# Moving the first layernorm's normalisation from GpSimd to VectorE and ScalarE in a linear-attention block with a gated MLP

## The chip, the cores and the metric

The kernel runs on one core of a Trainium2 chip. The metric is the device time of one execution in microseconds; the median of several runs is compared. The core has TensorE (PE, matrix products), VectorE (DVE), ScalarE (ACT), GpSimd (POOL) and SyncE (SP, which only issues DMAs here). TensorE writes its products to eight PSUM banks; the others bring them from there to on-chip memory (SBUF).

## What is computed

```python
def _layernorm(x, axis=-1, eps=1e-5):
    m = jnp.mean(x, axis=axis, keepdims=True)
    v = jnp.var(x, axis=axis, keepdims=True)
    return (x - m) / jnp.sqrt(v + eps)

def _A_ref(x, wqkv, wo):                      # H = 32 heads of 32
    q, k, v = ...                             # x @ wqkv, split
    phi = lambda t: jnp.where(t > 0, t + 1, jnp.exp(t)) + 1e-6
    pq, pk = phi(q), phi(k)
    kv = jnp.einsum("bhsd,bhse->bhde", pk, v)
    z = jnp.einsum("bhsd->bhd", pk)
    num = jnp.einsum("bhqd,bhde->bhqe", pq, kv)
    den = jnp.einsum("bhqd,bhd->bhq", pq, z)[..., None] + 1e-6
    return merge_heads(num / den) @ wo

def _B_ref(x, W_gate, W_up, W_down):
    gate = jnp.einsum("bsd,df->bsf", x, W_gate)
    up = jnp.einsum("bsd,df->bsf", x, W_up)
    gate = gate * (gate > 0)
    return jnp.einsum("bsf,fd->bsd", gate * up, W_down)

h  = x + _A_ref(_layernorm(x), wqkv, wo)
h2 = h + _B_ref(_layernorm(h), W_gate, W_up, W_down)
```

There are 2048 tokens of width 1024, and the hidden width of the MLP is 3584. All inputs and the output are bf16.

## The kernel before

**Stages.** The tokens are cut into tiles of 128 rows, 16 in all. The first layernorm (class `Norm`, L644) takes them in pairs: tile t of the first half of the tokens and tile t + 8 of the second. K and V are computed pair by pair, and K^T V is accumulated in PSUM (the K/V stage). The Q stage follows, together with the attention tiles (class `Tile_`, L1004): each divides by the denominators, multiplies by wo, adds x, and applies the second layernorm. Then come gate and up, then down.

**Products.** Most products use a fast scheme with seven products in place of eight on 2x2 blocks (class `Quad`, L326). It needs sums and differences of blocks of the left operand (`left_sums`, L621) and of the weights (`WForms.sums`, L596, and others), all made by VectorE. A quad takes three PSUM banks A, D and E. p1 writes A, and ScalarE copies it to D (`fork`). p6 adds to A, and ScalarE copies the result out (`snap`, u2). p5 writes E; p7 adds to A, and that is copied out too (u3). p2 adds to D. Then an output is made from E and u3 (c22), and only when E has been read may p3 add to it. p4 adds to A. p4 and p3 of a quad are issued after p1 of the next.

**The first layernorm.** Its statistics are computed in two ways. Most tiles of the first half use VectorE (`bn_stats`, `bn_aggr`). Tiles with `on_act` use ScalarE: a Copy pass whose accumulator gives the sum, then, once the negated mean is known, a Square pass with that as its bias, whose accumulator gives the variance. `neg` (L656) computes the negated mean on GpSimd, for both kinds. `rstd_` (L678) does Ln and Exp on ScalarE. `finish` (L696) applies the two: GpSimd does (x + (-mean)) * rstd for twelve tiles, VectorE for tiles 1 and 9. Tiles 0 and 8 have their own path (`apply_first`, L685), with the mean itself, on VectorE. A DMA transpose then puts the tile into XI, from where TensorE reads it. The second layernorm (`Tile_.norm`, L1074) has its own code and applies on GpSimd.

**The order of the work.** The program is not issued as it is written. Class `Plan` (L33) records every instruction as a node with its predecessors, an estimated duration (`hold`) and a due time (`late`, from TensorE's order and the successors). `schedule` (L202) then runs a list schedule on a clock of its own, in nanoseconds, and the instructions are issued in that order; on the chip each engine takes its own in order. On an engine other than TensorE the ready node with the earliest due time is taken; but the engine may be held idle for a node that is not yet ready, if that becomes ready within a part of the candidate's duration and is due more than 1500 ns earlier. That part is `(1.2 if s < self.SHORT else 0.5) * v.hold` (L246), with `SHORT = 215000.0` on the planner's clock.

**The attention tiles.** `tiles` (L1089) lists 16 of them; `steps` (L1094) makes the program's order from the list, one tile behind another. Index `i` is the half of the tokens, `s` the half within that, `tt` the tile within 512 columns. The first eight (s = 0) run during the Q stage, and their second layernorm must be in XI before the first gate products. In `norm` a tile with i = 1 also asks for left sums: with tt = 1 for columns 0 and 1 together (four sums of 128x1024), with tt = 2 and 3 for one each (four of 128x512).

Of the kernel before, what the change touches and what calls it, by code (L numbers as in the profile page):

```python
# [8 lines left out]
ACT = mybir.ActivationFunctionType  # L9
ALU = mybir.AluOpType  # L10
# [22 lines left out]
class Plan:  # L33
# [6 lines left out]
    WINDOW = 6000.0  # L40
    AHEAD = 120000.0
    OPENING = 45000.0
    SHORT = 215000.0

    class Node:
        __slots__ = ("eng", "calls", "preds", "hold", "lat", "open", "dma", "late", "ready", "left", "start", "nom")
# [155 lines left out]
    def schedule(self):  # L202
        nodes = self.nodes
        succs = self.order()
        engines = ("tensor", "vector", "scalar", "gpsimd", "sync")
        avail = {e: [] for e in engines}
        clock = {e: 0.0 for e in engines}
        for i, v in enumerate(nodes):
            v.left, v.ready = len(v.preds), max(0.0, v.late - self.AHEAD) if v.dma else 0.0
            if v.eng != "tensor" and v.late > 2.0 * self.OPENING:  # L210

                v.ready = max(v.ready, self.OPENING)
            if not v.left:
                avail[v.eng].append(i)
        pe = [i for i, v in enumerate(nodes) if v.eng == "tensor"]
        done, first, wire, out = set(), 0, 0.0, []
        while True:
            best = None
            for e in engines:
                a = avail[e]  # L220
                if not a:
                    continue
                if e == "sync":
                    for i in a:
                        v = nodes[i]
                        if v.late - max(clock[e], v.ready) > 6000.0:
                            v.ready = max(v.ready, wire - 2000.0)
                if e == "tensor":
                    while first < len(pe) and pe[first] in done:
                        first += 1  # L230
                    limit = nodes[pe[first]].nom + self.WINDOW
                    a = [i for i in a if nodes[i].nom <= limit]
                    if not a:
                        continue
                s = max(clock[e], min(nodes[i].ready for i in a))
                if best is None or s < best[0]:
                    best = (s, e, a)
            if best is None:
                break
            s, e, a = best  # L240
            now = [i for i in a if nodes[i].ready <= s]
            i = min(now, key=lambda i: (nodes[i].nom if e == "tensor" else nodes[i].late, i))
            v = nodes[i]
            if e != "tensor":

                wait = (1.2 if s < self.SHORT else 0.5) * v.hold  # L246
                soon = [j for j in a if s < nodes[j].ready < s + wait and nodes[j].late < v.late - 1500.0]
                if soon:
                    i = min(soon, key=lambda j: (nodes[j].late, j))
                    v = nodes[i]  # L250
                    s = v.ready
            v.start = s
            clock[e] = s + v.hold
            end = s + v.hold + v.lat
            if v.dma:
                wire = max(wire, s + v.hold) + v.dma
                end = wire + v.lat - v.dma + min(4000.0, max(0.0, 0.25 * (v.late - s)))
            elif e == "sync":

                end = max(end, min(wire + 800.0, end + 2500.0))  # L260
            avail[e].remove(i)
            done.add(i)
            out.append(i)
            for j in succs[i]:
                w = nodes[j]
                r = clock[e] if w.eng == e else end
                w.ready = max(w.ready, r)
                w.left -= 1
                if not w.left:
                    avail[w.eng].append(j)  # L270
        assert len(out) == len(nodes)
        self.span = max(clock.values())
        return out
# [205 lines left out]
def block_kernel(ctx: ExitStack, tc: tile.TileContext, x, wqkv, wo, wg, wu, wd, out, H: int):  # L479
    nc = tc.nc  # L480
    P = 128
    xf = x.flatten_outer_dims()
    of = out.flatten_outer_dims()
    S, D = xf.shape
# [9 lines left out]
    SW = 512  # L494
    NS = 2
# [45 lines left out]
    def scratch(tag, n):  # L541

        if tag not in tiny_rings:
            tiny_rings[tag] = [0, tiny_at[0]]
            tiny_at[0] += 4 * n
            assert tiny_at[0] <= 208
        r = tiny_rings[tag]
        r[0] += 1
        lo = r[1] + (r[0] % 4) * n
        return tiny[:, lo:lo + n]  # L550
# [16 lines left out]
    hw, nc = nc, Plan(nc)  # L567
# [69 lines left out]
    def load_x(t):  # L637
        p, i = t % NP, t // NP
        x_tiles[t] = at(190 + 4 * (p % 2) + 2 * i, [D])
        nc.sync.dma_start(out=x_tiles[t], in_=xf[t * P:(t + 1) * P, :])  # L640
# [3 lines left out]
    class Norm:  # L644
# [8 lines left out]
            else:  # L653
                self.stats = scratch("stats", 2 * 6).rearrange("p (a b) -> p a b", b=6)

        def neg(self, src, by):  # L656
            self.negm = scratch("negm", 1)
            nc.gpsimd.tensor_scalar(out=self.negm[:], in0=src, scalar1=by, scalar2=None, op0=ALU.mult)

        def stat(self, j):  # L660
            if not self.on_act:
                nc.vector.bn_stats(out=self.stats[:, j, :], in_=self.x[:, j * 512:(j + 1) * 512])
            elif j == 0:
                nc.scalar.activation(out=self.xn, in_=self.x, func=ACT.Copy, accum_out=self.sm[:, 0:1])
                self.neg(self.sm[:, 0:1], -1.0 / D)
            else:
                nc.scalar.activation(out=self.xn, in_=self.x, func=ACT.Square, bias=self.negm[:], scale=1.0,
                                     accum_out=self.sm[:, 1:2])

        def aggr(self, first=False):  # L670
            if self.on_act:
                return
            self.mv = mv = scratch("mv", 2)
            nc.vector.bn_aggr(out=mv[:], in_=self.stats[:])
            if not first:
                self.neg(mv[:, 0:1], -1.0)

        def rstd_(self):  # L678
            lnv = scratch("lnv", 1)
# [13 lines left out]
            for k in range(2):  # L693
                nc.scalar.copy(out=XH[self.i][k][:, :, self.r:self.r + P], in_=pt[:, k * KH:(k + 1) * KH, :])

        def finish(self, on_dve=False):  # L696
            self.rstd_()
            xn = self.xn
            (nc.vector if on_dve else nc.gpsimd).tensor_scalar(out=xn, in0=self.x, scalar1=self.negm[:], scalar2=self.rstd[:],
                                    op0=ALU.add, op1=ALU.mult)  # L700
            nc.sync.dma_start_transpose(out=XI[self.i][:, :, self.r:self.r + P], in_=xn)
            if self.t == ST - 1:
                nc.follow(nc.last())
                for k, h in W_ORDER:
                    WQ.load(k, h)
                nc.follow(None)
            if self.t % NP + 2 < NP:
                load_x(self.t + 2)
# [83 lines left out]
    def v_quad(p):  # L792
        v = v_ring()

        def blk(i, j):
            return v[:, i, j * KH:(j + 1) * KH, 0:P]

        def copy(i, j):
            return lambda ps: nc.scalar.copy(out=blk(i, j), in_=split(ps))

        def add(i, j):
            return lambda ps, u: nc.vector.tensor_tensor(out=blk(i, j), in0=split(ps), in1=split(u), op=ALU.add)

        return v, Quad(tok_prod(p, WV), fork, snap,
                       {"c11": copy(0, 0), "c12": add(0, 1), "c21": copy(1, 0), "c22": add(1, 1)}, five_banks)
# [31 lines left out]
    def plain_k(i, j):  # L837
        k_phi(i, j, plain(WK, i, j))
# [38 lines left out]
    n0, n8, n1, n9 = Norm(0), Norm(8), Norm(1), Norm(9, True)  # L877
    for n in (n0, n8):
        n.stat(0)
        n.stat(1)  # L880
        n.aggr(first=True)
        n.rstd_()
        n.apply_first()
    n0.transpose_first()
# [4 lines left out]
        n.stat(1)  # L889
        n.aggr()  # L890
    plain_k(0, 0)
    n1.finish(True)
    n9.finish(True)
    tick.bg.extend(ks)
    tick()
    plain_k(1, 0)
# [15 lines left out]
    for p in range(1, NP):  # L912
# [6 lines left out]
        v, vq = v_quad(p)  # L919
# [166 lines left out]
                return (lag_s[0], chain_of(*left_sums(self.s * SW + (self.tt + 1 - n) * P, n * P)))  # L1086

    lag_s, turned = [3], []
    tiles = [Tile_(s, i, tt) for s in range(NS) for tt in range(SW // P) for i in range(2)]  # L1089

    def w(m, j):
        return lambda: tiles[m].wo(j)
# [440 lines left out]
@with_exitstack  # L1533
def kernel(
    ctx: ExitStack,
    tc: tile.TileContext,
    A_x: bass.AP,
    A_wqkv: bass.AP,
    A_wo: bass.AP,
    B_x: bass.AP,  # L1540
    B_W_gate: bass.AP,
    B_W_up: bass.AP,
    B_W_down: bass.AP,
    out: bass.AP,
):
    block_kernel(tc, A_x, A_wqkv, A_wo, B_W_gate, B_W_up, B_W_down, out, H=32)
# [30 lines left out]
```

## Time and profile before

| What | us |
|---|---|
| median of 8 runs | 726.82 (726.63 to 726.96) |
| the profiled execution, device time | 726.68 |
| its span, first to last instruction | 724.9 |

Every group of instructions has the same line (L123, the helper that issues recorded calls), so groups are told apart by engine, operation and shape. Some groups around the layernorm, over the whole span: count, busy us, mean ns of one.

| Engine and operation | Count | Busy us | Mean ns |
|---|---|---|---|
| POOL TENSOR_SCALAR 128x1024 (both layernorms) | 28 | 40.9 | 1461 |
| POOL TENSOR_SCALAR 128x1 (negated means) | 14 | 5.1 | 364 |
| DVE TENSOR_SCALAR 128x1024 with tiny operands | 4 | 2.2 | 546 |
| ACT ACTIVATE 128x1, tiny from tiny | 64 | 12.7 | 202 |

Busy time in windows of the first part, us:

| Window | PE | DVE | ACT | POOL |
|---|---|---|---|---|
| 20 to 40 | 18.58 | 17.53 | 15.49 | 8.13 |
| 40 to 60 | 18.07 | 15.30 | 14.86 | 8.60 |
| 60 to 80 | 20.00 | 15.77 | 16.10 | 5.91 |
| 80 to 100 | 20.00 | 14.55 | 10.29 | 0.81 |

The first layernorm's GpSimd applications run from 25.6 to 80.8 us and those of the second from 159.2 us on.

### The profile page before, as it was taken

The page shows a single profiled execution, that of the slowest core. Times are in us where ns is not written, and L with a number is a line of the kernel's source. Part 1 is how long each engine was busy: PE and PEld are TensorE (multiplying, and loading weights), DVE is VectorE, ACT ScalarE, POOL GpSimd, SP SyncE. Part 2 cuts the span into 40 slices and gives each one's busy share as a digit, 9 for nine tenths or more (in the row PEclk, how much of TensorE's full clock was granted, in tenths as well). Part 3 has the DMA queues.
Part 4 walks back from the last instruction along what each step waited for, and adds up shares of the span by engine and source line. Part 5 has one row for each costly group of instructions (what it writes and reads, how often), then busy time and mean ns, then how long its engine had stood idle before and what let it go on. Part 6 is the DMA issues. An engine that isn't in the chain of part 4 may idle for free.

```text
span 724.9 us, 11231 instructions
## 1 busy us (share of the span) xinstructions
PE 714.0 (98%) x4163; PEld 396.9 (55%) x4163; DVE 566.3 (78%) x954; ACT 277.2 (38%) x540; POOL 81.6 (11%) x88
## 2 busy tenths in 40 slices
PE   8998999999999999999999999999999999999998
PEld 3444545444444444444444444444444688888887
DVE  6887765788897965566766968769858879899996
ACT  5777654665655343333333333333333220001100
POOL 1343100002201220000000000000000004001452
PEclk9999999999999999999999999999999999999999
DMA  9544805249955540446145584686681868777973
GB/s 290 145 91 101 199 2 185 50 93 211 203 119 146 131 102 1 128 141 182 59 144 180 171 257 139 205 254 185 200 262 51 276 263 207 218 265 237 245 78 59
DMA packets 156503, 117.40 MB, mean 162 GB/s; under 512 B 54944, under 2 KB 140192, under 8 KB 156320
## 3 DMA queue, kind: packets, MB, share of 16 engines
q1 hardware_dynamic: 148832, 113.01, 53.5%
q0 software_dynamic: 7616, 3.67, 4.8%
q8 instruction: 32, 0.52, 0.3%
q14 instruction: 23, 0.19, 0.1%
HBM read 70.52 MB, written 34.08 MB: 144 GB/s over the span
## 4 chain that ended last, share of the span: by engine, by line
PE 87%; DVE 2%; ACT 2%; issue 1%; DMA 0%; POOL 0%; ACTq 0%; DVEq 0%
PE psum L123 87%; DVE mem L123 2%; ACT mem L123 1%; DMA mem<-mem 0%; ACT tiny L123 0%; ACT psum L123 0%; DVE tiny L123 0%; POOL tiny L123 0%; ACTq L123 0%; DVEq L123 0%
## 5 line engine op out<-in xcount | busy, mean ns | idle before, releaser
L123 PE MATMUL psum<-mem 128*128 128x512 bf16 (+4 forms) x4147 | 713.1, 335 | 7.4 <-ACT mem L123 2.6
L123 PEld LDWEIGHTS <-mem 128*128 128x128 f16 (+1 forms) x4163 | 396.9, 98 | 324.1 <-issue 10.8
L123 DVE TENSOR_TENSOR mem<-psum,mem 128x512 f32<-128x512 f32 (+2 forms) x240 | 187.1, 793 | 102.2 <-ACT mem L123 71.0
L123 DVE TENSOR_TENSOR mem<-mem 128x512 f16<-128x512 bf16 (+8 forms) x400 | 244.0, 650 | 7.9 <-DMA mem<-mem 2.8
L123 ACT COPY mem<-psum 128x512 f32<-128x512 f32 (+2 forms) x124 | 92.8, 750 | 215.3 <-PE psum L123 211.1
L123 ACT COPY psum<-psum 128x512 f32<-128x512 f32 (+1 forms) x68 | 49.1, 722 | 158.3 <-PE psum L123 156.1
L123 POOL DMA_DIRECT2D out_dram<-mem x28 | 34.1, 1299 | 412.1 <-DVE mem L123 412.0
L123 POOL TENSOR_SCALAR mem<-mem,tiny 128x1024 bf16<-128x1024 bf16 x28 | 40.9, 1461 | 181.7 <-ACT tiny L123 168.8
L123 ACT ACTIVATE mem<-psum 128x512 bf16<-128x512 f32 x90 | 53.6, 597 | 18.8 <-PE psum L123 18.2
L123 DVE SCALAR_TENSOR_TENSOR mem<-mem 128x512 bf16<-128x512 bf16 (+1 forms) x71 | 57.3, 806 | 1.2
L123 DVE SCALAR_TENSOR_TENSOR mem<-psum,mem 128x512 bf16<-128x512 f32 x66 | 45.2, 687 | 12.5 <-PE psum L123 10.2
L123 DVE TENSOR_SCALAR mem<-mem 128x512 bf16<-128x512 bf16 (+1 forms) x49 | 17.2, 354 | 19.9 <-ACT mem L123 19.3
L123 ACT ACTIVATE mem<-mem,tiny 128x1024 bf16<-128x1024 bf16 x24 | 27.5, 1145 | 8.4 <-DVE tiny L123 5.9
L123 DVE TENSOR_TENSOR mem<-psum,tiny 128x384 bf16<-128x384 f32 (+1 forms) x48 | 22.8, 507 | 4.3 <-ACT tiny L123 3.9
L123 ACT ACTIVATE mem<-mem 128x1024 bf16<-128x1024 f32 (+1 forms) x23 | 24.3, 1056 | 2.9 <-DVE mem L123 2.7
L123 ACT ACTIVATE tiny<-tiny 128x1 f32<-128x1 f32 (+2 forms) x112 | 22.5, 206 | 6.6 <-DVE tiny L123 3.8
L123 ACT ACTIVATE tiny<-psum 128x12 f32<-128x12 f32 (+1 forms) x48 | 8.1, 170 | 17.5 <-PE psum L123 17.2
L123 DVE BATCH_NORM_STATS2 tiny<-mem 128x6 f32<-128x512 bf16 x16 | 10.3, 683 | 2.4 <-DMA mem<-in_A_x_dram 2.4
L123 ACT CAST mem<-psum 128x512 bf16<-128x512 f32 x18 | 10.6, 588 | 4.2 <-PE psum L123 3.7
L123 POOL TENSOR_SCALAR tiny<-tiny 128x1 f32<-128x1 f32 x14 | 5.1, 364 | 38.8 <-ACT mem L123 21.4
L123 ACT ACTIVATION_READ_ACCUMULATOR mem<-mem,tiny 128x1 f32 x24 | 4.5, 188 | 0.0
L123 DVE TENSOR_SCALAR mem<-mem,tiny 128x1024 bf16<-128x1024 bf16 x4 | 2.2, 546 | 2.1 <-ACT tiny L123 1.5
(18 smaller groups left out, 15.6 us busy)
## 6 DMA issues: line engine op xcount, KB each, us to landing
l_dram<-mem SPq DMA_DIRECT2D x98, 128.0 KB, 2.3
mem<-l_dram SPq DMA_DIRECT2D x12, 896.0 KB, 6.3
mem<-in_A_x_dram SPq DMA_DIRECT2D x32, 256.0 KB, 3.0
mem<-in_B_W_up_dram SPq DMA_DIRECT2D x14, 512.0 KB, 5.4
mem<-in_B_W_gate_dram SPq DMA_DIRECT2D x14, 512.0 KB, 4.3
mem<-in_B_W_down_dram SPq DMA_DIRECT2D x28, 256.0 KB, 3.7
r_dram<-mem SPq DMA_DIRECT2D x56, 128.0 KB, 2.0
mem<-r_dram SPq DMA_DIRECT2D x8, 896.0 KB, 5.3
```

The costliest lines, as they stand in the source:

```text
L123: call = lambda: getattr(getattr(self.nc, eng), op)(*args, **k)
```

## The change

Four things. The hold of 1.2 durations applies only between 120 and 215 us of the planner's clock; before 120 us it is 0.5, as it already was after 215. The negated mean of the `on_act` tiles is computed by ScalarE, as a Copy with a scale; the other tiles use the mean itself and subtract. VectorE applies all tiles of `finish`. And the first eight attention tiles run all of i = 0 first, then all of i = 1, in place of alternating.

```diff
-    SHORT = 215000.0
+    MIXED = (120000.0, 215000.0)
...
-                wait = (1.2 if s < self.SHORT else 0.5) * v.hold
+                wait = (1.2 if self.MIXED[0] < s < self.MIXED[1] else 0.5) * v.hold
...
-        def neg(self, src, by):
-            self.negm = scratch("negm", 1)
-            nc.gpsimd.tensor_scalar(out=self.negm[:], in0=src, scalar1=by, scalar2=None, op0=ALU.mult)
-
         def stat(self, j):
             if not self.on_act:
                 nc.vector.bn_stats(out=self.stats[:, j, :], in_=self.x[:, j * 512:(j + 1) * 512])
             elif j == 0:
                 nc.scalar.activation(out=self.xn, in_=self.x, func=ACT.Copy, accum_out=self.sm[:, 0:1])
-                self.neg(self.sm[:, 0:1], -1.0 / D)
+                self.negm = scratch("negm", 1)
+                nc.scalar.activation(out=self.negm[:], in_=self.sm[:, 0:1], func=ACT.Copy, scale=-1.0 / D)
...
-        def aggr(self, first=False):
+        def aggr(self):
             if self.on_act:
                 return
             self.mv = mv = scratch("mv", 2)
             nc.vector.bn_aggr(out=mv[:], in_=self.stats[:])
-            if not first:
-                self.neg(mv[:, 0:1], -1.0)
...
-        def finish(self, on_dve=False):
+        def finish(self):
             self.rstd_()
             xn = self.xn
-            (nc.vector if on_dve else nc.gpsimd).tensor_scalar(out=xn, in0=self.x, scalar1=self.negm[:], scalar2=self.rstd[:],
-                                    op0=ALU.add, op1=ALU.mult)
+            by, op = (self.negm[:], ALU.add) if self.on_act else (self.mv[:, 0:1], ALU.subtract)
+            nc.vector.tensor_scalar(out=xn, in0=self.x, scalar1=by, scalar2=self.rstd[:], op0=op, op1=ALU.mult)
             nc.sync.dma_start_transpose(out=XI[self.i][:, :, self.r:self.r + P], in_=xn)
...
-    tiles = [Tile_(s, i, tt) for s in range(NS) for tt in range(SW // P) for i in range(2)]
+    tiles = [Tile_(0, i, tt) for i in range(2) for tt in range(SW // P)]
+    tiles += [Tile_(1, i, tt) for tt in range(SW // P) for i in range(2)]
```

More of the change, by code (lines that the diff above doesn't have):

```diff
@@ L880, in block_kernel @@
         n.stat(1)
-        n.aggr(first=True)
+        n.aggr()
         n.rstd_()
@@ L891, in block_kernel @@
     plain_k(0, 0)
-    n1.finish(True)
-    n9.finish(True)
+    n1.finish()
+    n9.finish()
     tick.bg.extend(ks)
```

## The prediction

> **What bounds the kernel now.** I read the page's list of busy times first, then TensorE's waits, its timeline, and the other engines around the two long gaps.
>
> ```profile
> PE 714.0 (98%) x4163; PEld 396.9 (55%) x4163; DVE 566.3 (78%) x954; ACT 277.2 (38%) x540; POOL 81.6 (11%) x88
> ```
> ```profile
> PE psum L123 <- ACT mem L123: 2.6, 2, 1.9
> PE psum L123 <- DVE mem L123: 2.1, 3, 1.4
> PE psum L123 <- DVE mem L558: 1.2, 1, 1.2
> PE psum L123 <- DMA mem<-mem: 0.6, 1, 0.6
> ```
> TensorE is idle for 724.9 - 714.0 = 10.9 us, and no change of other engines can win more. 3.5 of these follow its last matmul (721.35 to 724.9), 1.2 precede the first. Its timeline (columns: start, duration, what, idle before) has the rest:
>
> ```profile
> 10.49 18.29 PE L123 MATMUL psum<-mem 128*128 128x512 bf16 x84 [0.42 <-DMA mem<-in_A_wqkv_dram]
> 30.20 25.34 PE L123 MATMUL psum<-mem 128*128 128x512 bf16 x140 [1.42 <-DVE mem L123]
> 57.47 4.69 PE L123 MATMUL psum<-mem 128*128 128x512 f16 x21 [1.93 <-ACT mem L123]
> ...
> 171.95 4.94 PE L123 MATMUL psum<-mem 128*128 128x512 bf16 x28 [0.35 <-DVE mem L123]
> 177.24 30.61 PE L123 MATMUL psum<-mem 128*128 128x512 bf16 x152 [0.35 <-DVE mem L123]
> ```
> So the first layernorm's stretch holds two gaps, 1.42 us before 30.20 and 1.93 us before 57.47; the Q stage holds small ones (0.58 before 152.08 and the two of 0.35). From 270 to 721 TensorE runs without one. The change is worth what it does to the first two, less what it opens elsewhere.
>
> The gap before 57.47, on ScalarE and then on GpSimd:
>
> ```profile
> 52.38 0.57 ACT L123 COPY mem<-psum 128x512 f32<-128x512 f32 x1
> 54.89 1.15 ACT L123 ACTIVATE mem<-mem,tiny 128x1024 bf16<-128x1024 bf16 x1 [1.94 <-POOL tiny L123]
> ...
> 57.31 0.60 ACT L123 COPY psum<-psum 128x512 f32<-128x512 f32 x1
> ```
> ```profile
> 50.30 4.38 POOL L123 TENSOR_SCALAR mem<-mem,tiny 128x1024 bf16<-128x1024 bf16 x2
> 54.65 0.20 POOL L123 TENSOR_SCALAR tiny<-tiny 128x1 f32<-128x1 f32 x1
> ```
> The Square pass waits for a negated mean of 0.20 us, which stands on GpSimd behind two applications of 4.38 us. Behind the Square stand the copies that release TensorE: the delay is passed on whole (1.94 against 1.93).
>
> The gap before 30.20, on VectorE:
>
> ```profile
> 27.28 2.06 DVE L123 TENSOR_TENSOR mem<-mem 128x2048 f16<-128x2048 bf16 x1
> 29.27 0.28 DVE L123 TENSOR_SCALAR mem<-mem 128x512 bf16<-128x512 bf16 x1
> 29.47 0.68 DVE L123 TENSOR_TENSOR mem<-psum,mem 128x512 f32<-128x512 f32 x1
> ```
> TensorE waits for the add at 29.47, which reads bank E before p3 may add to it. Its other input, the copy u3, ended on ScalarE at 27.68: the add is late because weight sums stand before it. The last took 2.06 us, where the others take 1.22, beside a GpSimd application (28.27 to 30.54).
>
> **What the Trainium skill says.** "SBUF — State Buffer", section "Who interferes with whom": a VectorE operation with two SBUF inputs and a GpSimd operation that reads SBUF exclude each other for a whole instruction. The trace agrees: 2.06 against 1.22, and GpSimd's applications take 1.20 to 2.68 us. "TensorE: Matmul & The Clock Gate", the table of specifications: ScalarE's and VectorE's queues are strict FIFO. The trace agrees (ScalarE's 1.94 us above). "ScalarE: Activation LUTs", "Rules for kernel authors": about 0.3 us for an ACTIVATE besides its elements; the trace has 0.20 for a 128x1 one, and I use that.
>
> **The change part by part.**
> 1. *Twelve applications go from GpSimd to VectorE.* GpSimd loses 19.9 us (twelve at 1.665 mean up to 130 us). On VectorE four such stand in the trace:
>
> ```profile
> L123 DVE TENSOR_SCALAR mem<-mem,tiny 128x1024 bf16<-128x1024 bf16 x4 | 2.2, 546 | 2.1 <-ACT tiny L123 1.5 <-issue 0.5
> ```
> From start to next start one takes 0.46 (11.93 to 12.39). 12 x 0.46 = 5.5 us more. Less contention gives back 2.06 - 1.22 = 0.84 at 27.28 and 0.93 - 0.29 = 0.64 at 41.49: 1.5. Net 4.0. From 20 to 80 us VectorE is busy 17.53 + 15.30 + 15.77 = 48.6 of 60 (windows of 20 us); 52.6 fits, but the first window goes to about 18 of 20. On the chain to the next tile's transpose, 0.55 replaces 1.2 to 2.7, so the transposes go out 1 to 2 us sooner; TensorE waits for none there.
> 2. *Seven negations move to ScalarE, seven vanish.* ScalarE gains 7 x 0.20 = 1.4 us on 46.5 of 60, but no longer waits for GpSimd. At 52.4: the Square can start about 53.1 (after the copy, which ends at 52.95, and a negation of 0.20), not 54.89: 1.8 us of the 1.93 go. What is late next is ScalarE's own chain (Square, Ln, Exp, fork). Bounds: 0, if another wait takes its place, to 1.93. I take 1.8.
> 3. *The shorter hold before 120 us of the planner's time.* It costs nothing on the chip: it changes the order in which instructions are issued. VectorE stands idle for 2.19 us before 20.34, waiting for a transpose, with weight sums still to do. A hold of 0.5 in place of 1.2 durations lets one in (1.14 from start to start, 26.15 to 27.28). The other way, a long sum may now start in front of an urgent add. The add at 29.47 then: -0.84 (contention) -1.14 (idle time filled) +0.92 (two applications, ready at 25.4 and 28.0, in front of it) = 28.4; that takes 1.1 us of the 1.42. Bounds: +0.9 (applications before it, idle not filled, contention elsewhere) to -1.42. I take -1.0.
> 4. *Order of the first eight attention tiles.* Same work, other order. Left sums of columns 0 and 1 wait for the sixth tile, not the fourth: four sums of 0.68 move from 180-186 to after 188, those of column 2 (four of 0.42) about 3 us later. First gate products use them from about 204. VectorE's idle time is 13.00 - 10.14 = 2.9 in 187-200 and 8.00 - 7.62 = 0.4 in 200-208. 2.7 us fit, barely. Bounds -0.7 (both gaps of 0.35 closed, as VectorE is freer before 187) to +1.5. I take +0.2.
> 5. *New small stalls* from a fuller VectorE with more waits in 20-80: VectorE now stops for each rstd, with bank releases queued behind it. I take +0.2; its bad end is the second rival. The SP queue has the same transposes and loads, earlier; nothing is added to it. GpSimd's accumulating stores come after 600 us.
>
> Sum: -1.8 - 1.0 + 0.2 + 0.2 = -2.4 us. The profiled execution took 726.68 (span 724.9 and 1.8 around it): 724.3, span 722.5. The median before, 726.82, lies 0.14 higher: 724.4.
>
> **Rivals.**
> *Only one gap closes.* The first stays at 1.4, because the applications take the place of the contention, or the second turns into a wait for VectorE; gain 1.8 less small stalls of 0.8: 725.8. For it: VectorE is at 88% in 20-40. Against: the second gap's cause is removed by name.
> *VectorE as the bound (slower).* An application at the head of its queue waits for Ln and Exp on ScalarE, with bank releases behind it. The row above prices it: 2.1 us idle before four, 0.53 each; 12 x 0.53 = 6.3. Idle time left is 7.4 of 60 us. If half of the stops fall before an add that TensorE needs (3.2) and both applications at 25-29 do (0.9), less the 1.8 won: +2.3, 729.1. It decides once TensorE loses more than 1.8 to such stops. For it: ScalarE is busy 9.27 of 10 us in 20-30. Against: before a free VectorE comes to them, most rstd are long done.
> *All closes.* Both gaps (3.35) and the two of 0.35: 726.82 - 4.05 = 722.8. For it: both causes named above lie in what is removed. Against: closing the first needs VectorE to be free in its tightest window.
>
> **How the numbers follow.** Forecast 0.50 (own range 723.3 to 725.4), one gap 0.18, VectorE as bound 0.22, all 0.10. A measurement of this kernel tells about 0.2% (1.45 us) from no change, so "same" is 725.4 to 728.3. Faster: 0.50 + 0.10 = 0.60; same: 0.18 and a little of the third, 0.19; slower 0.21. Range: the low end is below "all closes" by a little, 722.4; the high end takes in one gap and the mild part of the third case, 728.5.
>
> **What would show it.** In the profile after: GpSimd has 16 applications and no 128x1 ones; no weight sum of 2 us; no wait of ScalarE for GpSimd's tiny tiles; TensorE's gap near 57 gone, that near 30 at 0.4 or less; the Q stage's within 0.5 of now. A wait of VectorE for ScalarE's tiny tiles that grows by several us, with TensorE waiting for VectorE from 20 to 80 us, would make it wrong; so would a gap before the first gate products near 204.

## The result

The changed kernel takes 724.5 us (median of 11 runs, 724.24 to 725.51) against 726.77 for the kernel before (31 runs): a ratio of 0.997, with a 95% interval of 0.9963 to 0.9978. The prediction said 724.4. The profiled execution took 724.65 us, its span is 722.9.

The page of the kernel after, list of busy times:

```profile
PE 714.1 (99%) x4163; PEld 396.6 (55%) x4163; DVE 569.6 (79%) x966; ACT 277.8 (38%) x548; POOL 56.7 (8%) x62
```

TensorE has the same work in a span shorter by 2.0 us. VectorE gained only 3.3 us of busy time for twelve more applications; GpSimd lost 24.9 and has 16 applications left and no negations. TensorE's waits, in the kernel after (total us, times, longest):

```profile
PE psum L123 <- DVE mem L123: 1.2, 4, 0.4
PE psum L123 <- DVE mem L558: 1.2, 1, 1.2
PE psum L123 <- ACT mem L123: 0.9, 2, 0.7
PE psum L123 <- DMA mem<-mem: 0.8, 1, 0.8
```

And its timeline:

```profile
10.45 43.96 PE L123 MATMUL psum<-mem 128*128 128x512 bf16 x224 [0.71 <-DMA mem<-in_A_wqkv_dram]
54.60 14.16 PE L123 MATMUL psum<-mem 128*128 128x512 f16 x76 [0.20 <-ACT mem L123]
68.91 13.18 PE L123 MATMUL psum<-mem 128*128 128x512 bf16 x72 [0.15 <-DVE mem L123]
82.47 47.77 PE L123 MATMUL psum<-mem 128*128 128x512 bf16 x267 [0.38 <-DVE mem L123]
...
149.94 19.52 PE L123 MATMUL psum<-mem 128*128 128x512 bf16 x112 [0.77 <-DMA mem<-mem]
169.81 4.94 PE L123 MATMUL psum<-mem 128*128 128x512 bf16 x28 [0.35 <-DVE mem L123]
175.10 30.75 PE L123 MATMUL psum<-mem 128*128 128x512 bf16 x152 [0.34 <-DVE mem L123]
```

The gap of 1.42 us is no longer a row of its own: one run of products goes from 10.45 to 54.41. The one of 1.93 is now 0.20. Two small ones, 0.15 and 0.38, are new, and the two in the Q stage stand as before. Together these come to -1.42 - 1.73 + 0.15 + 0.38 = -2.6. The wait for the first attention tile's transpose grew from 0.58 to 0.77, which leaves -2.4. The product behind that wait was, in the kernel before:

```profile
152.08 19.52 PE L123 MATMUL psum<-mem 128*128 128x512 bf16 x112 [0.58 <-DMA mem<-mem]
```

From the first product of the long run (10.49 and 10.45) to this one (152.08 and 149.94), TensorE takes 141.59 us before and 139.49 after: -2.1. The missing 0.3 went into stalls too short to be listed: up to the second place the products count as 43.96 us busy, where before they counted 18.29 + 25.34 = 43.63. This distance, called the stretch below, leaves out the start of the execution, which differs from run to run.

ScalarE at the second place, in the kernel after:

```profile
51.14 0.19 ACT L123 ACTIVATION_READ_ACCUMULATOR mem<-mem 128x1 f32 x1
51.23 0.19 ACT L123 ACTIVATE tiny<-tiny 128x1 f32<-128x1 f32 x1
51.32 0.57 ACT L123 COPY mem<-psum 128x512 f32<-128x512 f32 x1
51.79 0.21 ACT L123 ACTIVATE tiny<-tiny 128x1 f32<-128x1 f32 x1
52.03 1.15 ACT L123 ACTIVATE mem<-mem,tiny 128x1024 bf16<-128x1024 bf16 x1
...
54.45 0.59 ACT L123 COPY psum<-psum 128x512 f32<-128x512 f32 x1
```

The accumulator is read at 51.14, and the Square pass starts 0.89 us later; before, it was 52.28 and 54.89, 2.6 us. A negation of about 0.2 us on ScalarE itself is all that lies between besides other ready work. VectorE at the first place, in the kernel after:

```profile
25.70 1.22 DVE L123 TENSOR_TENSOR mem<-mem 128x2048 f16<-128x2048 bf16 x1
26.83 0.54 DVE L123 TENSOR_SCALAR mem<-mem,tiny 128x1024 bf16<-128x1024 bf16 x1
27.29 0.69 DVE L123 BATCH_NORM_STATS2 tiny<-mem 128x6 f32<-128x512 bf16 x1
27.89 0.28 DVE L123 TENSOR_SCALAR mem<-mem 128x512 bf16<-128x512 bf16 x1
28.08 0.69 DVE L123 TENSOR_TENSOR mem<-psum,mem 128x512 f32<-128x512 f32 x1
```

The add on which p3 waits starts at 28.08, not 29.47; one application and a statistics pass stand before it, and the last weight sum takes its plain 1.22 and starts 1.58 sooner (25.70 for 27.28).

### The profile page after: what moved, and what is told of

The parts are those of the page before. It is cut to its first block, busy times and chain, and to the rows that moved or that the text cites. A ratio compares the mean times of both kernels' runs of the same rounds, so it can differ in the third digit from the quotient of the medians.

```text
span 722.9 us, 11207 instructions
## 1 busy us (share of the span) xinstructions
PE 714.1 (99%) x4163; PEld 396.6 (55%) x4163; DVE 569.6 (79%) x966; ACT 277.8 (38%) x548; POOL 56.7 (8%) x62
## 4 chain that ended last, share of the span: by engine, by line
PE 87%; DVE 6%; ACT 3%; DMA 2%; issue 1%; SPq 0%; ACTq 0%; DVEq 0%
PE psum L123 87%; DVE mem L123 6%; ACT mem L123 3%; DMA mem<-in_A_wqkv_dram 1%; DMA mem<-mem 1%; DVE tiny L123 1%; ACT tiny L123 1%; SPq L123 0%; ACT psum L123 0%; ACTq L123 0%; DVEq L123 0%
## 5 line engine op out<-in xcount | busy, mean ns | idle before, releaser
L123 POOL TENSOR_SCALAR mem<-mem,tiny 128x1024 bf16<-128x1024 bf16 x16 | 20.9, 1309 | 243.3 <-ACT tiny L123 243.3
L123 ACT ACTIVATE tiny<-tiny 128x1 f32<-128x1 f32 (+2 forms) x120 | 24.0, 205 | 8.3 <-DVE tiny L123 5.3
L123 DVE TENSOR_SCALAR mem<-mem,tiny 128x1024 bf16<-128x1024 bf16 x16 | 8.5, 542 | 3.1 <-ACT tiny L123 3.1
L123 DVE TENSOR_SCALAR tiny<-tiny 128x1 f32<-128x1 f32 x16 | 3.4, 210 | 0.4
```

The costliest lines, as they stand in the source:

```text
L123: call = lambda: getattr(getattr(self.nc, eng), op)(*args, **k)
```

## The experiments

The change mixes where an operation runs with the order in which everything is issued, since the planner reads the engine and the hold. To part the two, the first experiments keep a kernel's order of issue to the instruction and only exchange the engine at the moment of issue: a recorded call may carry a substitute.

```diff
+        instead = k.pop("instead", None)
-        call = lambda: getattr(getattr(self.nc, eng), op)(*args, **k)
+        call = lambda: instead(self.nc) if instead else getattr(getattr(self.nc, eng), op)(*args, **k)
```

All were timed beside the kernel before. The table has their median time and its ratio to the kernel before (95% interval), and the stretch in the one profiled execution of each. Kernels that differ from one another only in the attention tiles agree in the stretch within 0.05 us (before and tiles_only; changed, after_old_tiles and second_on_vector; hold_from_60 and hold_60_second_vector), so it resolves more than the medians do, but nothing outside 10 to 152 us.

| Kernel | us | Ratio to before | Stretch, us |
|---|---|---|---|
| before | 726.77 | 1 | 141.59 |
| changed | 724.50 | 0.9970 (0.9963 to 0.9978) | 139.49 |
| neg_same_order | 724.83 | 0.9971 (0.9959 to 0.9982) | 139.40 |
| apply_same_order | 724.83 | 0.9970 (0.9960 to 0.9980) | 139.59 |
| both_same_order | 724.81 | 0.9969 (0.9957 to 0.9981) | 139.55 |
| hold_only | 725.99 | 0.9986 (0.9980 to 0.9993) | 141.33 |
| tiles_only | 726.65 | 0.9999 (0.9991 to 1.0007) | 141.57 |
| after_old_hold | 724.59 | 0.9971 (0.9961 to 0.9981) | 139.72 |
| after_old_tiles | 724.70 | 0.9970 (0.9959 to 0.9982) | 139.46 |
| after_apply_gpsimd | 728.83 | 1.0028 (1.0018 to 1.0038) | 143.77 |
| after_neg_gpsimd | 724.62 | 0.9973 (0.9961 to 0.9984) | 139.61 |
| second_on_vector | 723.99 | 0.9959 (0.9947 to 0.9972) | 139.51 |
| hold_from_60 | 723.88 | 0.9960 (0.9948 to 0.9973) | 138.61 |
| hold_60_second_vector | 722.80 | 0.9947 (0.9934 to 0.9961) | 138.66 |

### The engines alone, in the old order

**neg_same_order**: only the negations of the tiles with statistics on ScalarE move to ScalarE.

```diff
-            nc.gpsimd.tensor_scalar(out=self.negm[:], in0=src, scalar1=by, scalar2=None, op0=ALU.mult)
+            nc.gpsimd.tensor_scalar(..., **(dict(instead=lambda e: e.scalar.activation(
+                out=out, in_=src, func=ACT.Copy, scale=by)) if self.on_act else {}))
```

> The order of issue is that of the kernel before, and only the seven negations of the tiles with statistics on ScalarE are issued on ScalarE in place of GpSimd. Theory A (each gap has its local cause: the negation behind two applications makes the gap before 57.47): that gap falls from 1.93 to under 0.3 us, the one of 1.42 before 30.20 stays within 0.3; the time falls by 1.5 to 1.9, to about 725.1. Rival B (the gain comes from the planner's new order, and a wait that is removed alone is replaced by the next): the gap is replaced by another of 1 us or more and the time falls by less than 0.5.

TensorE's timeline in neg_same_order (its lines bear L124, as the substitute added one):

```profile
13.66 15.92 PE L124 MATMUL psum<-mem 128*128 128x512 bf16 x72
30.91 99.40 PE L124 MATMUL psum<-mem 128*128 128x512 bf16 x541 [1.33 <-DVE mem L124]
```

The second gap is gone from the list and the first stands at 1.33. The time falls by 2.1, a little more than the 1.5 to 1.9 expected, and the stretch by 2.2: seven moved instructions of 0.2 us, in an unchanged order, bring about as much as the whole change. Rival B falls.

**apply_same_order**: the twelve applications move to VectorE, and all negations stay.

```diff
-            (nc.vector if on_dve else nc.gpsimd).tensor_scalar(out=xn, in0=self.x, ...)
+            (nc.vector if on_dve else nc.gpsimd).tensor_scalar(out=xn, in0=x, ...,
+                instead=lambda e: e.vector.tensor_scalar(out=xn, in0=x, ...))
```

> The order of issue is that of the kernel before; the twelve applications are issued on VectorE in place of GpSimd, all negations stay on GpSimd. Theory A: no weight sum of 2 us is left, the negation near 54 no longer stands behind applications, so the gap before 57.47 falls below 0.5; the gap before 30.20 changes by -0.8 (contention gone) to +0.9 (two applications in front of the add); the time falls by 1 to 2.5, to 724.3 to 725.8. Rival B: VectorE in the old order stops at applications whose rstd is late, TensorE waits for VectorE by 1 us or more in 20 to 80, and the time is 726.5 or more.

```profile
13.79 15.06 PE L124 MATMUL psum<-mem 128*128 128x512 bf16 x68
29.05 1.02 PE L124 MATMUL psum<-mem 128*128 128x512 f16 x4 [0.20 <-ACT mem L124]
30.75 99.49 PE L124 MATMUL psum<-mem 128*128 128x512 bf16 x540 [0.67 <-DVE mem L124]
```

This is the same timeline for apply_same_order. The second gap goes here too, though the negation is still on GpSimd: what held it there was the queue in front of it. Of the first gap 0.20 + 0.67 = 0.87 are left. Rival B, VectorE as the bound in the old order, falls.

**both_same_order** joins the two edits.

> The order of issue is that of the kernel before; the applications go to VectorE and the seven negations to ScalarE. Theory A: nearly all of the changed kernel's gain without any new order: 724.4 to 725.2, TensorE's idle time from 20 to 80 us at most 1.2 (3.35 before). Rival B (new order needed): 725.8 or more.

724.81, within 0.02 of each alone. The two edits do not add up, since either one removes the same cause of the second gap: a small instruction that others wait for, behind long ones on GpSimd. What the applications do to the first gap as well (a few tenths) is too small for the medians. The gap before 30 is 1.04 here. VectorE's part shows why it is 0.38 lower than before:

```profile
28.68 0.54 DVE L706 TENSOR_SCALAR mem<-mem,tiny 128x1024 bf16<-128x1024 bf16 x1
29.14 0.28 DVE L124 TENSOR_SCALAR mem<-mem 128x512 bf16<-128x512 bf16 x1
29.34 0.68 DVE L124 TENSOR_TENSOR mem<-psum,mem 128x512 f32<-128x512 f32 x1
29.94 0.54 DVE L706 TENSOR_SCALAR mem<-mem,tiny 128x1024 bf16<-128x1024 bf16 x1
```

The contention saves 0.84, and one application in front of the add (28.68 to 29.14) costs 0.46; the other comes after it.

### The order alone

**hold_only** and **tiles_only** are the kernel before with one of these edits each (as in the diff of the change).

> The kernel before with only the hold changed (0.5 before 120 us of the planner's clock), GpSimd as before. Theory A: the gap at 57 stays at 1.5 or more, since the negation still stands behind applications; the one at 30 falls by 0 to 1.1; 725.7 to 726.8. Rival B (the order is what gains): 725.3 or less.

```profile
29.65 25.68 PE L123 MATMUL psum<-mem 128*128 128x512 bf16 x137 [0.48 <-DVE mem L123]
56.78 21.49 PE L123 MATMUL psum<-mem 128*128 128x512 f16 x118 [1.45 <-ACT mem L123]
78.60 51.43 PE L123 MATMUL psum<-mem 128*128 128x512 bf16 x279 [0.32 <-DVE mem L123]
```

In hold_only the first gap falls by 0.94, the second only by 0.48 (to 1.45, just under the 1.5 expected), and a new one of 0.32 opens near 78: together -1.1. The median fell by 0.95, but this trace does not show that the one follows from the other. Its stretch is only 0.26 shorter than that of the kernel before, so some 0.8 us went into stalls too short to be listed; and the profiled execution, 726.71, is the second slowest of 21 (724.82 to 727.13). What lowers the median beyond 0.3 us stays open. Its VectorE is idle for 0.17 us before the first left sums, with a weight sum at 19.07, where the kernel before has 2.19:

```profile
19.07 1.22 DVE L123 TENSOR_TENSOR mem<-mem 128x2048 f16<-128x2048 bf16 x1
...
21.39 0.43 DVE L123 TENSOR_TENSOR mem<-mem 128x512 f16<-128x512 bf16 x1 [0.17 <-DMA mem<-mem]
```

> The kernel before with only the order of the first eight attention tiles changed. Theory A: +0.2, 727.0, both gaps in 20 to 60 unchanged. Rival C: 726.3 or less.

tiles_only is not told from the kernel before (0.9991 to 1.0007), and both gaps stand, at 1.40 and 1.92. The expected +0.2 is not seen.

### Parts taken back from the changed kernel

**after_old_hold** has the old hold, **after_old_tiles** the old order of tiles.

> The changed kernel with the old hold (1.2 up to 215 us of the planner's clock). Theory A: VectorE stands idle again for about 2 us before the first left sums near 20, so the add before p3 near 28 is late by about 1 us, or other urgent adds are served better; 724.0 to 725.6, a TensorE gap near 28 to 30 of 0.3 to 1.2. Rival C (the hold does nothing): within 0.3 of 724.5 and no such gap.

> The changed kernel with the attention tiles alternating as before. Theory A (the tile order costs +0.2 through left sums that come late): 724.3, TensorE's idle time from 140 to 220 lower by 0 to 0.5. Rival C (the tile order gains): 724.8 or more.

```profile
11.87 18.29 PE L123 MATMUL psum<-mem 128*128 128x512 bf16 x82 [0.58 <-DMA mem<-in_A_wqkv_dram]
31.10 26.21 PE L123 MATMUL psum<-mem 128*128 128x512 bf16 x141 [0.95 <-DVE mem L123]
57.88 92.95 PE L123 MATMUL psum<-mem 128*128 128x512 bf16 x505 [0.57 <-DVE mem L123]
151.59 19.52 PE L123 MATMUL psum<-mem 128*128 128x512 bf16 x110 [0.76 <-DMA mem<-mem]
```

With the old hold, the gap near 31 is back at 0.95 and there is one of 0.57 near 58; those near 69 and 82 are gone. VectorE is idle again for 2.29 us before its first left sums. Yet the median, 724.59, is not told from the changed kernel's. The profiled execution took 725.99, the longest of its eight runs, because it waited for weights for 1.07 and 0.58 us before 12 us: its long run starts at 11.87, not at 10.45. The stretch leaves that out, and is 139.72 against 139.49. So once the applications are on VectorE the short hold is worth about 0.2 us there, much as in the old kernel (0.26): most of what it wins near 30 it gives back in later stalls.

The tile order is not told from nothing here either: 724.70 lies between the two theories, and the gaps of 0.34 near 171 and 176 stay. From the product behind the first attention tile's transpose to the next gap near 207, TensorE takes 56.00 us in the kernel before, 55.98 in tiles_only, 56.14 in the changed kernel and 55.99 in after_old_tiles: whatever the order does there, it is under 0.2.

**after_apply_gpsimd**: the changed kernel's order, with the twelve applications issued on GpSimd again.

```diff
-            nc.vector.tensor_scalar(out=xn, in0=self.x, scalar1=by, scalar2=self.rstd[:], op0=op, op1=ALU.mult)
+            nc.vector.tensor_scalar(..., **(dict(instead=lambda e: e.gpsimd.tensor_scalar(out=xn, in0=x, ...))
+                if self.t not in (1, 9) else {}))
```

> The changed kernel's order of issue, but its twelve later applications are issued on GpSimd again (subtracting the mean there); negations stay on ScalarE. Theory A: contention stretches weight sums again (one or more of over 1.7 us between 20 and 30), but nothing on ScalarE waits behind applications; transposes go out 1 to 2 us later; 724.5 to 725.6. Rival B (the order carries the gain): within 0.3 of 724.5. Rival D (VectorE's new load was what made the two new gaps at 68.9 and 82.5): those two go, and the time is 724.2 or less.

Every theory missed: 728.83, 4.3 us slower than the changed kernel and 2 slower than the one before. TensorE's timeline in after_apply_gpsimd:

```profile
33.32 8.87 PE L124 MATMUL psum<-mem 128*128 128x512 f16 x51 [0.50 <-ACT mem L124]
43.47 17.66 PE L124 MATMUL psum<-mem 128*128 128x512 f16 x90 [1.28 <-ACT mem L124]
62.40 9.73 PE L124 MATMUL psum<-mem 128*128 128x512 f16 x55 [1.27 <-ACT mem L124]
72.88 13.18 PE L124 MATMUL psum<-mem 128*128 128x512 bf16 x71 [0.74 <-DVE mem L124]
87.45 42.79 PE L124 MATMUL psum<-mem 128*128 128x512 bf16 x239 [1.39 <-DVE mem L124]
```

One of its chains, on GpSimd, SyncE and ScalarE in turn:

```profile
33.80 4.05 POOL L698 TENSOR_SCALAR mem<-mem,tiny 128x1024 bf16<-128x1024 bf16 x1 [3.93 <-ACT tiny L124]
```
```profile
37.87 1.24 SPq L124 DMA_TRANSPOSE mem<-mem  x1
```
```profile
41.04 1.06 ACT L124 ACTIVATE mem<-mem 128x1024 bf16<-128x1024 bf16 x1 [1.68 <-DMA mem<-mem]
...
43.31 0.59 ACT L124 COPY psum<-psum 128x512 f32<-128x512 f32 x1
```

The application takes 4.05 us beside a full VectorE (the twelve take 2.49 on average). Its transpose goes out at 37.87 and lands at 40.93. The next statistics pass on ScalarE writes into a buffer of the ring of three which that transpose reads, so it waits; behind it in ScalarE's queue stands the fork that releases TensorE. VectorE in its turn waits 5.5 us for transposes from 20 to 100 us, against 2.9 in the changed kernel. The gap before 62.40 comes the same way, behind a wait of 2.18 us at 60.49. The one before 87.45 follows VectorE's longest wait for a transpose (2.71 at 84.31), and the one before 72.88 a VectorE instruction of 0.98 us beside GpSimd, where others of its shape take 0.28. So the order made for VectorE counts on applications of half a microsecond, and a slow GpSimd breaks it, mostly through late transposes and the buffers that they hold.

**after_neg_gpsimd**: the changed kernel's order, with only the seven negations back on GpSimd.

> The changed kernel's order of issue, only the seven negations issued on GpSimd again; the applications stay on VectorE. Theory A (what cost time was the negation behind applications, not GpSimd's negation itself): within 0.4 of the changed kernel, ScalarE's waits for GpSimd under 0.5 each. Rival E (each trip to GpSimd and back costs ScalarE enough to move TensorE): 0.6 or more slower than the changed kernel.

724.62; ScalarE's only wait for them from 20 to 100 us is one of 0.6 (under 0.5 was expected), and the stretch grows by 0.1. Rival E falls: the trip to GpSimd costs next to nothing, once nothing long stands in its queue.

### A better version

**hold_from_60** lets the hold of 1.2 begin at 60 us of the planner's clock; **second_on_vector** has VectorE apply the second layernorm too; the last has both.

```diff
-    MIXED = (120000.0, 215000.0)
+    MIXED = (60000.0, 215000.0)
...
-            nc.gpsimd.tensor_scalar(out=self.hn, in0=self.h, scalar1=self.negm[:], scalar2=rstd[:],
+            nc.vector.tensor_scalar(out=self.hn, in0=self.h, scalar1=self.negm[:], scalar2=rstd[:],
```

> The changed kernel with the hold of 1.2 from 60 us of the planner's clock, not 120. Theory A (the short hold closes the gap near 28 and opens those near 69 and 82): the first stays closed, the two of 0.15 and 0.38 go, the time falls by 0.3 to 0.6. Rival C: the two gaps have another cause and stay; within 0.2.

```profile
54.84 93.71 PE L123 MATMUL psum<-mem 128*128 128x512 f16 x518 [0.19 <-ACT mem L123]
```

In hold_from_60 TensorE runs from 54.84 to 148.55 without a listed gap: the short hold had made those near 69 and 82, with the applications on VectorE in both kernels. The time is 723.88, and the stretch falls by 0.9.

> The changed kernel with the second layernorm's 16 applications on VectorE too. If the sums stretched to 1.15 beside GpSimd make the two gaps of 0.35 near 170 and 175, these close and the time falls by 0.3 to 0.9; if VectorE's own new work in the same places takes the stretch's room, the gaps stay and the time is within 0.3 or, from 200 to 220 where VectorE is at 97%, worse by up to 1.

In the changed kernel a sum beside a GpSimd application takes 1.15 us and the evacuation at 169.07, for which TensorE waits, starts late:

```profile
168.00 1.15 DVE L123 TENSOR_TENSOR mem<-mem 128x1024 f16<-128x1024 bf16 x1
169.07 0.68 DVE L123 SCALAR_TENSOR_TENSOR mem<-psum,mem 128x512 bf16<-128x512 f32 x1
```

In second_on_vector the application itself stands there, at half the length, and the evacuation waits only for TensorE's product:

```profile
168.34 0.54 DVE L123 TENSOR_SCALAR mem<-mem,tiny 128x1024 bf16<-128x1024 bf16 x1
168.93 0.69 DVE L123 SCALAR_TENSOR_TENSOR mem<-psum,mem 128x512 bf16<-128x512 f32 x1
```

Both gaps of 0.35 close; one near 207 grows from 0.23 to 0.44. The time is 723.99. The planner has also moved the sum away from there, since it reads the engine; what the engine does and what the order does were not parted here.

> Both of the last two edits. If their gains are of different gaps (0.15 and 0.38 near 69 and 82; those in the Q stage), they add up: 1.1 to 1.3 below the changed kernel, near 723.3, a ratio of about 0.995 to the kernel before; if one shares the other's room, 723.8.

722.80: 1.7 below the changed kernel, where the two edits alone give 0.6 and 0.5. They add up; the further 0.5 is within the runs' scatter (0.9934 to 0.9961). It is the fastest of all by its median.

## Why the prediction was right, and where it was off

- *Second gap, -1.8 from the negations on ScalarE.* Right in size and cause: 1.93 to 0.20 in the changed kernel, 2.1 us of time for that edit alone in the old order. What the prediction did not see is that part 1 by itself removes the same wait, so that parts 1 and 2 are not terms of a sum; after_neg_gpsimd shows it from the other side.
- *First gap, -1.0 from contention and idle time, less applications.* No listed gap is left: -1.4. The contention of 0.84 is shown: with the order unchanged and only the applications moved, the sum takes 1.21 (27.55 in both_same_order). The prediction named the wrong application beside it. The sum started at 27.28, before the one at 28.27; what held it up was the one before, from 25.59 to 28.27. The one at 28.27 was itself held up by the sum, and ended 1.20 us after it (29.34, 30.54). Only one application stood before the add, at +0.46, not two at +0.92, but also a statistics pass at +0.60 that the prediction did not have. VectorE's idle time was filled as argued: 2.19 to 1.04 in the changed kernel, to 0.17 in hold_only. The rest of the add's 1.39 is one small instruction fewer in front of it (0.33) and an earlier end of the idle time (0.12). The filled idle time is a gain at this place alone: over the stretch the short hold is worth 0.2.
- *Tile order, +0.2.* Not told from nothing in either direction, within about 0.6 us in the old order, and under 0.2 in the traces where the tiles run; its bounds of -0.7 to +1.5 were wider than needed.
- *New small stalls, +0.2, from a fuller VectorE.* They came, at 0.53 (0.15 and 0.38), but from the short hold: hold_from_60 keeps the load and has none of them, and hold_only has one of 0.32 without the load. The cause given in that step was wrong, and the size too small by 0.3, without the stalls too short to be listed. Those seem to come from the short hold too: the stretch of hold_from_60 is 0.9 shorter, more than the two gaps make up.
- *The rival of a VectorE that stops for each rstd.* It does not decide: VectorE waits for ScalarE's tiny tiles 3.1 us before all sixteen applications, 0.19 each in place of the 0.53 that the rival took, and TensorE waits for VectorE 1.2 us in all after the start. "All closes" would have needed the Q stage's two gaps, which close only where VectorE applies the second layernorm too (second_on_vector, hold_60_second_vector).
- *The expected slack.* The prediction said that transposes going out 1 to 2 us sooner were worth nothing to TensorE. In the old order that holds (neg_same_order, with the applications on GpSimd, and both_same_order take the same time); in the new order after_apply_gpsimd loses 4.3 us, and three of its gaps (1.28, 1.27 and 1.39) stand behind late transposes.
- *The total.* -2.4 was forecast and -2.3 measured. The mechanism of the two gaps is right, but that the sum came so near is partly luck: the first gap gave 0.4 more than taken and the tile order cost nothing for 0.2, while the new stalls took 0.3 more, those too short to be listed another 0.3, and the wait for the first attention tile's transpose 0.2 that no term had.

## What to carry to other kernels

Before moving heavy work off an engine, look at what else stands in its queue: a small instruction that others wait for, behind long ones, may be the whole cost, and moving it alone is the cheaper cure. Two edits that cut the same chain are not two gains. A listed gap that closes is not yet a gain: measure between the same two products in both traces, which counts the short stalls too and leaves out the start (10.45 to 11.87 us here). Where a planner orders the work by engine and duration, test a move both in the old order and in the new one, since a schedule made for a short operation can depend on it through buffers far from where it stands.

## What was not expected of the hardware

A 128x1024 application on GpSimd, 1.19 us by itself, took 4.05 us beside a busy VectorE (33.80 in after_apply_gpsimd), and 4.82 at the worst (63.79). The same meeting stretched VectorE's sums in other places: 0.68 to 1.15 (168.00 in the changed kernel). The prediction had the two exclude each other for a whole instruction. That fits the meeting at 27.28 to 30.54 in the kernel before, where each waits for the other's end. It does not explain the one at 33.80. There four sums with both inputs in SBUF began and ended within the application's 4.05 us, so the application stood back for them; and yet one of them took 1.22 in place of 0.42 (34.30), so it stood back too. The loss can fall on either engine or on both; which of them it falls on, and when, stays open.
